# Moving two Strassen products of the last Q unit between the attention tiles of a fused transformer block

## The chip, the cores and the metric

The kernel runs on one core of one Trainium2 chip. The metric is the device time of one execution in microseconds (us). Most executions agree within 0.3%. "Granted clock" below is the mean clock that the throttle gave TensorE in one execution, as a share of full speed. With one core there is no second die to compare with, so a run counts as fast unless it is over 1.5% above the fastest of its kernel; all runs here were fast, apart from one single run whose state is unknown and that is used only for its trace.

## The reference, cut to what matters

```python
def _A_ref(x, wqkv, wo):                 # linear attention, S = 2048, D = 1024, 32 heads
    q, k, v = split(x @ wqkv)
    phi = lambda t: where(t > 0, t + 1, exp(t)) + 1e-6
    pq, pk = phi(q), phi(k)
    kv = einsum("bhsd,bhse->bhde", pk, v)
    z = einsum("bhsd->bhd", pk)
    o = einsum("bhqd,bhde->bhqe", pq, kv) / (einsum("bhqd,bhd->bhq", pq, z)[..., None] + 1e-6)
    return merge_heads(o) @ wo
# _B_ref: (relu(x @ W_gate) * (x @ W_up)) @ W_down, F = 3584
h   = x + _A_ref(layernorm(x), wqkv, wo)
out = h + _B_ref(layernorm(h), W_gate, W_up, W_down)
```

Only the middle of this matters here: Q = layernorm(x) @ wq with phi on it, then for each tile of 128 tokens numerator and denominator ("nd"), the division, the projection with wo, the residual, the second layernorm, and the first products of the FFN.

## The kernel before

All large products are made with seven block products in place of eight (Strassen's scheme in Winograd's form). One *unit* of Q makes two 128-column stripes `v` of the four quadrants. A generator hands out the unit in six pieces, so that the caller can put other work between them. Bank `A` accumulates products 1, 6, 7, 4; bank `E` accumulates 5 and 3. `snap` is a ScalarE copy of a bank as it stands, `fin(i, j, ...)` adds a copy to a bank and starts phi on quadrant (i, j); i = 0 is the first half of the rows. The scheme also needs sums of blocks of its operands, made on VectorE: *left sums* of the tokens and *weight sums* of the weights.

```python
def strassen(pool, work, mm, fin, sbufs=3):
    ...
    yield                                    # products 1, then 2 and 6, came first
    for v in range(2):
        E[v] = pool.tile([P, NW], FP32, tag="E", bufs=2, name="Eq")
        mm(E[v], 5, v, True)
    yield
    for v in range(2):
        mm(A[v], 7, v, False)
        snap(v, "u3")
        fin(1, 1, v, E[v], snaps["u3", v])
    yield
    for v in range(2):
        mm(A[v], 4, v, False)
        fin(1, 0, v, A[v], None)
    yield
    for v in range(2):
        mm(E[v], 3, v, False)
        fin(0, 1, v, E[v], snaps["u2", v])
    yield
```

The second half of the tokens has two Q units, twelve pieces. They are dealt over the eight attention steps 0 to 7. A step runs nd of one tile, the DMA transpose of the quotient of the tile before (`oT`), the projection of the tile two back (`wo_h`), and the DMA transpose and left sums of the tile four back. The first FFN *quad* (`flow`), an early block of the gate and up products by the same scheme, begins in step 8; it reads the sums of tiles 0 to 7. The Q unit that is last feeds tiles 8 to 15: its first-half quadrants tiles 8 to 11, its second-half quadrants tiles 12 to 15.

```python
LAG = (0, 1, 1, 2, 4)                    # nd, oT, x_in, wo_h, hn_T
rest = [p for s in range(1, NS) for c in range(0, KH, 2) for p in [q_unit(s, c)] * 6]
for step in range(QSTEPS):               # QSTEPS = 8
    now = rest[step * len(rest) // QSTEPS:(step + 1) * len(rest) // QSTEPS]
    if step == QSTEPS - 1:
        while now:
            next(now.pop(0))
    attn_step(step)
    ...                                  # early loads of FFN weights
    for p in now:
        next(p)
...
for step in range(QSTEPS, ready):        # steps 8 to 11
    if step == QSTEPS:
        flow.pop(0)()                    # weight sums and first product of FFN quad 0
    attn_step(step)
for n in range(steps):                   # then the rest of flow between the other steps
    attn_step(ready + n)
    ...
```

## Time and profile before

| | before |
|---|---|
| time, median of 3 runs (lowest to highest) | 743.94 us (742.64 to 744.77) |
| span of the profiled execution, granted clock | 740.6 us, 1.0 |
| TensorE (PE) busy | 721.8 us, 97% |
| PE busy of the 127 us from 165 to 292 (attention and early FFN) | 119.98 us |
| start of the first product 5 of FFN quad 0 | 220.34 us |
| start of the later FFN stage (first `accA` product) | 291.11 us |

Read it from the bottom: TensorE does the same matmuls whatever their order, so what can be won is the idle time in the third to last row, 7 us. From 292 us on there is next to none, so the start of `accA` tells nearly the whole of what an edit in this stage does to the end. The lines that carry this are in the prediction.

### The profile page before, as it was taken

To read this page: it belongs to the slowest core of one execution; us is meant where nothing else is said; L and a number is where in the kernel's file an instruction comes from. 1 tells how busy PE (TensorE), PEld (TensorE's weight loads), DVE (VectorE), ACT (ScalarE), POOL (GpSimd) and SP (SyncE) were. 2 spreads that over 40 slices of the span, in tenths; PEclk is the share of its full clock that TensorE was granted. 3 is DMA by queue.
4 is the path that set the end of the run, shared out by engine and by line. 5 is a ranking of instruction groups with operands and counts; after the bars stand their busy time and mean duration, and the time that the engine had idled before them with its cause. 6 is when DMAs were issued, how large, how long until landed. Compare 5 with 4: busy or idle time off the path is not lost.

```text
span 740.6 us, 10570 instructions
## 1 busy us (share of the span) xinstructions
PE 721.8 (97%) x3967; PEld 382.0 (52%) x4020; DVE 563.2 (76%) x991; ACT 322.0 (43%) x580; POOL 5.7 (1%) x44
## 2 busy tenths in 40 slices
PE   7999999999989999999999999999999999999997
PEld 3444555444444444444444444444444458888666
DVE  6997653675887767778778777877787479996797
ACT  4786553778686654444344434443435120000000
POOL 0000000000000000000000000000000000000000
PEclk9999999999999999999999999999999999999999
DMA  9765003079797526164638359475483399988822
GB/s 319 167 140 157 0 1 107 9 155 242 152 223 165 138 73 203 46 181 137 196 127 233 109 181 288 162 221 201 170 271 127 124 396 345 326 286 298 300 79 79
DMA packets 146579, 132.03 MB, mean 178 GB/s; under 512 B 50912, under 2 KB 128096, under 8 KB 146528
## 3 DMA queue, kind: packets, MB, share of 16 engines
q1 hardware_dynamic: 135392, 123.23, 55.3%
q10 hardware_dynamic: 11136, 8.13, 3.4%
q8 instruction: 31, 0.51, 0.3%
q14 instruction: 20, 0.16, 0.1%
HBM read 79.95 MB, written 39.85 MB: 162 GB/s over the span
## 4 chain that ended last, share of the span: by engine, by line
PE 78%; DVE 8%; ACT 7%; DMA 5%; issue 2%; SPq 0%; DVEq 0%; POOL 0%; ACTq 0%
PE accA L785 22%; PE accX L785 8%; PE accY L785 8%; PE accA L1117 8%; PE Aq L298 3%; PE accA L946 3%; PE accX L1117 3%; PE Aq L438 3%; DMA hn<-hn 2%; PE accY L1117 2%; PE attn L541 2%; PE Aq L705 2%; PE Eq L298 2%; PE accY L946 2%; PE accX L946 2%
## 5 line engine op out<-in xcount | busy, mean ns | idle before, releaser
L795 ACT ACTIVATE gu<-gu 128x512 bf16<-128x512 bf16 x72 | 45.4, 631 | 131.5 <-DVE gu L794 131.5
L790 ACT COPY snap<-accA 128x1024 f32<-128x1024 f32 x72 | 72.5, 1008 | 36.3 <-PE accA L785 36.2
L785 PEld LDWEIGHTS <-tg 128*128 128x128 f16 x384 | 37.6, 98 | 45.3
L785 PEld LDWEIGHTS <-tu 128*128 128x128 f16 x384 | 37.6, 98 | 45.3
L541 PE MATMUL attn<-wo_mem,oT 128*128 128x512 bf16 x249 | 57.9, 379 | 1.2 <-DVE o_sb L518 0.4
L794 DVE TENSOR_TENSOR gu<-accY,snap 128x1024 bf16<-128x1024 f32 x36 | 43.9, 1219 | 10.0 <-ACT snap L790 10.0
L785 PE MATMUL accA<-hn,tu 128*128 128x512 f16 (+1 forms) x192 | 49.3, 379 | 0.0
L785 PE MATMUL accA<-hn,tg 128*128 128x512 f16 (+1 forms) x192 | 49.3, 379 | 0.0
L794 DVE TENSOR_TENSOR gu<-accX,snap 128x1024 bf16<-128x1024 f32 x36 | 43.9, 1219 | 6.2 <-PE accX L785 3.7
L154 ACT COPY u<-Aq 128x512 f32<-128x512 f32 x56 | 32.4, 582 | 37.3 <-PE Aq L298 19.3
L1117 PEld LDWEIGHTS <-x 128*128 128x128 f16 (+1 forms) x448 | 43.8, 98 | 5.5
L785 PEld LDWEIGHTS <-wg 128*128 128x128 bf16 x288 | 28.2, 98 | 34.0
L785 PEld LDWEIGHTS <-wu 128*128 128x128 bf16 x288 | 28.2, 98 | 34.0
L541 PEld LDWEIGHTS <-oT 128*128 128x128 bf16 x256 | 24.6, 98 | 30.8 <-issue 2.9
L798 DVE TENSOR_TENSOR hq<-gu 128x512 bf16<-128x512 bf16 x48 | 20.3, 423 | 14.3 <-ACT gu L795 14.2
L298 PEld LDWEIGHTS <-xT 128*128 128x128 bf16 (+1 forms) x192 | 18.6, 98 | 23.7 <-issue 2.3
L1117 PEld LDWEIGHTS <-xs 128*128 128x128 f16 x280 | 27.4, 98 | 3.2
L543 DVE SCALAR_TENSOR_TENSOR x_res<-attn,x_res 128x512 bf16<-128x512 f32 x32 | 21.8, 687 | 7.2 <-PE attn L541 7.1
L946 PEld LDWEIGHTS <-x 128*128 128x128 bf16 (+1 forms) x168 | 16.4, 98 | 19.6
L518 DVE TENSOR_TENSOR o_sb<-nd,rd 128x384 bf16<-128x384 f32 (+1 forms) x48 | 22.8, 507 | 4.5 <-ACT rd L517 4.4
L1123 DVE TENSOR_TENSOR snap<-accA,u 128x1024 f32<-128x1024 f32 x16 | 19.5, 1220 | 8.3 <-PE accA L1117 8.0
L785 PE MATMUL accA<-hn,wu 128*128 128x512 bf16 x96 | 24.6, 379 | 0.0
(232 smaller groups left out, 1400.8 us busy)
## 6 DMA issues: line engine op xcount, KB each, us to landing
x<-x_dram SPq DMA_DIRECT2D x17, 896.0 KB, 8.2
x_dram<-hq SPq DMA_DIRECT2D x28, 512.0 KB, 3.1
wg<-in_B_W_gate_dram SPq DMA_DIRECT2D x14, 512.0 KB, 5.2
wu<-in_B_W_up_dram SPq DMA_DIRECT2D x14, 512.0 KB, 7.3
wraw<-in_B_W_down_dram SPq DMA_DIRECT2D x14, 512.0 KB, 4.8
x_dram<-hq SPq DMA_DIRECT2D x28, 256.0 KB, 2.6
t_dram<-wt SPq DMA_DIRECT2D x28, 256.0 KB, 2.2
xd<-x_dram SPq DMA_DIRECT2D x6, 896.0 KB, 7.1
```

Source lines behind the costliest of these rows:

```text
L154: nc.scalar.copy(out=snaps[nm, v], in_=A[v][:])
L298: nc.tensor.matmul(ps[:], lhsT=left[m - 1][:, kc, r + v * P:r + (v + 1) * P], rhs=right[m - 1][:, kc, :], start=(start and kc == 0), stop= ...
L438: nc.tensor.matmul(ps[:], lhsT=rq[m - 1][:, kc, (c + v) * P:(c + v + 1) * P], rhs=left[m - 1][:, kc, :], start=(start and kc == 0), stop=( ...
L518: nc.vector.tensor_tensor(out=ov[:, c0:c0 + n], in0=ndv[:, :, 0:P].rearrange("p k (h e) -> p k h e", h=HPC), in1=rd[:, 0:n, :].unsqueeze(3 ...
L541: nc.tensor.matmul(ps[:], lhsT=st["oT"][:, c, :], rhs=wo_sb[:, c, j * NW:(j + 1) * NW], start=(c == 0), stop=(c == KC - 1))
L543: nc.vector.scalar_tensor_tensor(out=h_sb[:, j * NW:(j + 1) * NW], in0=ps[:], scalar=1.0, in1=h_sb[:, j * NW:(j + 1) * NW], op0=ALU.mult, ...
L785: nc.tensor.matmul(ps[:, v, :], lhsT=w[v][n - 1][:, kc, :], rhs=left[n - 1][:, kc, :], start=(t is not None and kc == 0), stop=(kc == KH - ...
L790: nc.scalar.copy(out=st[nm][:], in_=halves(st["A"]))
L794: add(out=g[:], in0=halves(st[nm]), in1=st[base][:], op=ALU.add)
L795: nc.scalar.activation(out=g[:, 0, :], in_=g[:, 0, :], func=ACT.Relu)
L946: nc.tensor.matmul(ps[:, t * NW:(t + 1) * NW], lhsT=x_tile(n, s, kh)[:, f, (t0 + t) * P:(t0 + t + 1) * P], rhs=w_tile(n, kh)[:, f, :], sta ...
L1117: nc.tensor.matmul(pv[:, tt, :], lhsT=left(m)[:, f, tt * P:(tt + 1) * P], rhs=right(m)[:, f, :], start=(t is not None and f == 0 and tt % ...
```

## The change

In the last Q unit the first-half quadrants are formed first (products 1, 2, 6, 5, 3), and the two products that only the second-half quadrants need, 7 and 4, are held back to follow attention steps 8 and 9. The intent is to let the tiles of attention start earlier and to give TensorE independent work between them, where it ran dry before. Since product 3 now accumulates onto bank `E` ahead of product 7, product 5 is copied first. The FFN quad begins two steps later.

```diff
-    def strassen(pool, work, mm, fin, sbufs=3):
+    def strassen(pool, work, mm, fin, sbufs=3, late=False):
...
             mm(E[v], 5, v, True)
+            if late:
+                snap(v, "e5", E)
         yield
+        if late:
+            for v in range(2):
+                mm(E[v], 3, v, False)
+                fin(0, 1, v, E[v], snaps["u2", v])
+            yield
+            for v in range(2):
+                mm(A[v], 7, v, False)
+                fin(1, 1, v, A[v], snaps["e5", v])
+            yield
+            for v in range(2):
+                mm(A[v], 4, v, False)
+                fin(1, 0, v, A[v], None)
+            yield
+            return
...
+    last = rest[-2:]
+    del rest[-2:]
     for step in range(QSTEPS):
...
+    for step in range(QSTEPS, QSTEPS + 2):
+        attn_step(step)
+        next(last.pop(0))
...
-    for step in range(QSTEPS, ready):
-        if step == QSTEPS:
+    for step in range(QSTEPS + 2, ready):
+        if step == QSTEPS + 2:
             flow.pop(0)()
```

More of the change, by code (lines that the diff above doesn't have):

```diff
@@ L142, in hold, with snap @@
         nc.gpsimd.tensor_copy(out=dst, in_=src)
-    def strassen(pool, work, mm, fin, sbufs=3):
+    def strassen(pool, work, mm, fin, sbufs=3, late=False):
         A, E, snaps = {}, {}, {}
-        def snap(v, nm):
+        def snap(v, nm, bank=A):
             if v == 0:
@@ L153, in snap @@
             with tc.high_priority():
-                nc.scalar.copy(out=snaps[nm, v], in_=A[v][:])
+                nc.scalar.copy(out=snaps[nm, v], in_=bank[v][:])
         def m2(v):
@@ L447, in fin @@
                 phi_end(pair, e[:])
-        return strassen(pspool, qw[-1], mm, fin)
+        return strassen(pspool, qw[-1], mm, fin, 3, s == NS - 1 and c + 2 == KH)
     with tc.tile_pool(name="qwork0", reuse_waits="tile", bufs=2, side="right") as pool:
```

## The prediction

> **What bounds the kernel now.** I read the page first: TensorE (PE) is busy 97% of the span, and no other engine is near that.
>
> ```profile
> span 740.6 us, 10570 instructions
> PE 721.8 (97%) x3967; PEld 382.0 (52%) x4020; DVE 563.2 (76%) x991; ACT 322.0 (43%) x580; POOL 5.7 (1%) x44
> ```
>
> The reader is to see that all that can be won by moving work, and not removing any, is 740.6 - 721.8 = 18.8 us of idle PE, less than 3%. Next I cut the span by stage (columns: window, its length, busy us and instructions of each engine, clock, DMA share, GB/s).
>
> ```profile
> 120.00:165.00 45.00, 44.76 (x249) 22.00 (x252) 30.45 (x64) 29.95 (x63) 1.05 (x4) 1.00 0.41 106
> 165.00:292.00 127.00, 119.98 (x607) 56.47 (x618) 95.02 (x241) 87.64 (x218) 0.84 (x4) 1.00 0.72 171
> 292.00:580.00 288.00, 286.74 (x1312) 130.61 (x1335) 220.90 (x406) 123.80 (x165) 0.00 (x0) 1.00 0.55 175
> ```
>
> The second row is the attention stage with the second half's Q products and the first early FFN quads: 7.0 us idle. The FFN stage after it has only 1.3 us idle, so whatever reaches it earlier carries through. In ten-microsecond windows the hole is at 210 to 220, where PE is busy 7.28. The timeline of PE there (start, length, line, what; in brackets the idle time before and what ended it; L541 output projection, L511 numerator and denominator "nd", L705 early FFN quad):
>
> ```profile
> 211.75 0.52 PE L511 MATMUL nd<-kvz,pq_mem 128*128 128x132 bf16 x6
> 212.11 0.38 PE L705 MATMUL Dq<-hn,wg 128*128 128x512 bf16 x1
> 212.74 0.28 PE L511 MATMUL nd<-kvz,pq_mem 128*128 128x132 bf16 x2 [0.25 <-DVE o_sb L518]
> ...
> 213.34 3.61 PE L541 MATMUL attn<-wo_mem,oT 128*128 128x512 bf16 x15
> 216.79 0.51 PE L511 MATMUL nd<-kvz,pq_mem 128*128 128x132 bf16 x6
> 218.06 0.28 PE L511 MATMUL nd<-kvz,pq_mem 128*128 128x132 bf16 x2 [0.76 <-DVE o_sb L518]
> 220.34 0.59 PE L705 MATMUL Eq<-hs,tg 128*128 128x512 f16 x2 [2.00 <-DVE hs L117]
> ```
>
> PE has run out of work and waits 0.25, 0.76 and 2.00 us. The last wait is for the sums of token tile 7, the last of the eight that the first FFN quad needs. The chain of waits says where those came from:
>
> ```profile
> 210.50 1.24 ACT hn L553 x2
> 211.84 0.14 ACT sm L554
> 212.01 0.21 ACT sm L555
> 212.24 0.30 ACT sm L556
> 212.57 1.24 ACT hn L557
> 213.81 0.32 ACT den L515 x2
> ...
> 215.62 4.21 DMA hn<-hn
> 219.85 0.44 DVE hs L117
> ```
>
> Normalise (ACT), queue, transpose by DMA, sum (DVE): from the end of tile 7's projection, 207.6 by the PE timeline, to 220.34 it is 12.8 us. PE cannot shorten this chain; it can only start it earlier or have work beside it.
>
> A balance I use below: from the first Q matmul (122.2) to 220.34 are 98.1 us. In them PE does 224 Q matmuls, 160 of projection and 12 of the early quad, 396 x 0.216 us (eight take 1.73 us in the chain) = 85.5 us, and 13 tiles x 8 nd matmuls x 0.059 us (eight take 0.47 us) = 6.1 us. So 91.6 us of work and **6.5 us of idle**: 3.0 in the three waits above, 1.1 where PE waits for an ACT copy at 186.3, 0.3 for a transpose at 203.8, the rest in crumbs.
>
> **What the Trainium skill says.** (1) "TensorE: Matmul & The Clock Gate", in "Wait — 56ns, not 53.3ns?", has warm 512-column matmuls at 215.7 ns start to start; this trace agrees: 1.73 us for eight. (2) "PSUM — Partial Sum Buffer", in "Engine vs sequencer instructions": the queues of ScalarE and VectorE are strict FIFO and matmuls start in program order. So the order of the program decides who waits behind whom; I see nothing in the trace against it. (3) The same page, "PSUM bank collisions raise a hardware error", wants accesses of two engines to one bank guarded by semaphores, ACT reads against PE writes too. Before, product 4 continues on the bank that ACT must first copy; the trace shows that wait, 1.10 us on PE at 186.28 released by the copy. (4) "Perfetto Trace Analysis", in "Per-instruction lifecycle: what the profiler-reported window actually captures": on DMAs the data movement lies outside the slice. Agreed here: the transposes of hn show 1.23 us in the SP queue but 3.2 to 5.1 us to landing, median 3.9 in this stretch. I use the landing.
>
> **The change, part by part.** Nothing is added or removed on PE: its order lists 8042 rows in both kernels.
> - In the last Q unit the order of products becomes 1, 2, 6, 5, 3, 7, 4. ACT copies product 5 (two copies of 0.58 us) instead of the sum before product 7 (two of 0.58): net zero. The exponentials, clamps and adds stay the same in number.
> - Moved: products 7 and 4, 16 matmuls x 0.216 = **3.45 us of PE**, from before attention step 7 to after steps 8 and 9. They feed only tiles 12 to 15, whose nd comes later, so the data allows it.
> - The first early quad begins two steps later (its first product, 8 matmuls, 1.73 us).
>
> I compared the built PE orders. Up to the end of tile 7's projection PE has 82.4 us of work before and 79.0 after: product 4 and the first FFN product (together 3.45) are now behind it. Up to the first product-5 matmul of the quad, where the 2.00 us wait was, both have the same 91.6 us. So after the change PE holds 91.6 - 79.0 = 12.6 us of work beside the tile-7 chain, where before it held 91.6 - 82.4 = 9.2 beside a chain of 12.8.
>
> How long is the chain in its new place? ACT's new order puts two things into it: Square of tile 7 stands behind the two ACT reads of product 4 (done about 2.4 us after the projection ends, where the square could have started at some 1.6), and two FFN copies and one exponential (2 x 0.58 + 1.14 = 2.3 us) come inside. My estimate, from the projection's end: square until 3.6, copies 4.7, exponential and small steps 7.0, normalise 8.2, queue 9.0, landing (3.9) 12.9, sum 0.44: 13.3 us. Minus 12.6 leaves a wait of 0.7 us where 3.0 was: **2.3 us gained**.
>
> Other terms: the 1.1 us copy wait loses its reason in this unit (product 4 now follows long after), but product 3 must now wait for ACT's copy of product 5, and the second of those copies stands behind a square of tile 4: I put +0.3 to +0.5 on it. Tile 8's nd now follows product 3 by 4.1 us of PE work instead of 7.8, while its chain (two DVE adds 1.4, exponential 1.1, clamp 0.4, maximum 0.7, plus hand-overs) is about as long: up to 0.5 us lost. Together +0.2 us gain. Sum: 2.5 us, 743.9 - 2.5 = **741.4 us**.
>
> **Rivals.** (a) *The wait only moves.* Steps 8 to 11 are spaced 4 to 5 us in the trace; with two hn buffers, each square waits for the transpose of two tiles earlier ((3.3 ACT + 1.5 queue + 4 DMA)/2 = 4.4 us). If that ring, and not PE, sets the pace, the filler fits beside it but the tiles come no sooner, and the wait in front of product 5 stays near 2 us: 743.3. For it: DMA share is 1.0 at 160 to 180 and again at 200 to 220. Against it: tile 7 starts 3.45 us of PE work earlier, and tiles 4 to 6 are spaced 4 to 7 us there. (b) *ACT becomes the bound.* It is busy 8.2 to 8.8 of 10 us at 160 to 190, and PE gives up 3.45 us of cover in just those steps, though ACT also gives up some 3.7 us (two exponentials, two reads). If PE then waits for ACT all through steps 3 to 7, the gain halves: 742.7. (c) *It all comes off.* The copy wait goes and the chain is fully covered: 4 us, 739.9. (d) *A slip later.* The early quads after 220 have their own 3.0 us of idle (70.9 us from 220.34 to the first accA matmul, 67.9 of work); the reshuffled order could add one. That would make it 744 to 745.
>
> **Range and chances.** Between (c) and (a) lies 739.7 to 743.7, which I take as the range: low end everything won, high end nearly nothing. Faster by 2% would be 729, more than 14 us gained of 18.8 idle: about nil. Slower by 2% needs 15 us of new waits: nil. So faster 0.01, same 0.98, slower 0.01.
>
> **What would show it right or wrong.** Right: in the changed profile the wait before the first Eq matmul of the early quad is under 1 us, that matmul starts near 217.8 instead of 220.3, PE busy at 210 to 220 rises from 7.3 to above 9, and the start of the first accA product moves from 291.3 to about 288.8. Rival (a) shows as 1.5 us or more in front of that matmul, released by DVE sums that waited for hn; (b) as new PE waits on ACT copies or on nd's inputs between 160 and 200; (d) as more than 3.5 us of idle between that matmul and accA. The prediction is wrong if the gain is there at 220 but not at the end, or if tile 8's nd waits over 1 us.

## More of the kernel before

One more pair of lines from before's timeline of TensorE (start, length, engine, line, what, count) is needed later. They are the projections of tiles 3 and 4; a count of 15 is 16 with one record missing.

```profile
175.27 3.62 PE L541 MATMUL attn<-wo_mem,oT 128*128 128x512 bf16 x15
...
187.57 3.62 PE L541 MATMUL attn<-wo_mem,oT 128*128 128x512 bf16 x16
```

They start 12.3 us apart. Between them PE does most of products 6 and 4, half of 2 and the whole of 5 and 7 of the last Q unit.

## The result, and the profile after

| | before | after |
|---|---|---|
| median (lowest to highest), 4 runs each | 743.38 (742.64 to 744.77) | 740.18 (739.59 to 740.64) |
| ratio of fast runs, 95% interval | 1 | 0.9954 [0.9936, 0.9972] |
| span of the profiled execution | 740.6 | 738.4 |

A ratio is the mean time of one kernel's fast runs over that of the other's of the same rounds, so it is not quite the ratio of the medians. The change gains 0.5%, which is "same" at 2% but clear of zero. Results are correct.

The head of the page after the change:

```profile
span 738.4 us, 10554 instructions
...
PE 722.7 (98%) x3967; PEld 382.2 (52%) x4020; DVE 562.9 (76%) x991; ACT 323.0 (44%) x580; POOL 5.6 (1%) x44
```

TensorE's work is the same; the span is 2.2 us shorter. By stage (window, its length, busy us and instructions of PE, PEld, DVE, ACT, POOL, granted clock, DMA share, GB/s):

```profile
165.00:292.00 127.00, 122.33 (x618) 57.58 (x629) 96.17 (x243) 89.72 (x220) 1.11 (x4) 1.00 0.72 171
210.00:220.00 10.00, 7.69 (x46) 3.70 (x45) 10.00 (x31) 9.16 (x29) 0.00 (x0) 1.00 0.75 133
```

The first row has 2.35 us more PE work in the same window than before. The second shows something that was not forecast: PE is no fuller than before (7.69, from 7.28), and VectorE (DVE), which was busy 7.81 of these 10 us, is now busy for all 10. The timeline of PE after the change says what PE did there (L454 Q products, L527 nd, L557 projection, L726 early FFN quad, L806 the later FFN stage; `x_res` is the residual add, `o_sb` the quotient of a tile, `hs` a left sum):

```profile
156.34 3.61 PE L557 MATMUL attn<-wo_mem,oT 128*128 128x512 bf16 x15 [0.53 <-DVE o_sb L534]
...
170.55 1.89 PE L557 MATMUL attn<-wo_mem,oT 128*128 128x512 bf16 x8 [0.20 <-DVE o_sb L534]
...
176.99 3.62 PE L557 MATMUL attn<-wo_mem,oT 128*128 128x512 bf16 x15
...
182.16 3.61 PE L557 MATMUL attn<-wo_mem,oT 128*128 128x512 bf16 x16
...
202.94 1.89 PE L454 MATMUL Aq<-xT,tq 128*128 128x512 bf16 x8
...
212.09 0.59 PE L557 MATMUL attn<-wo_mem,oT 128*128 128x512 bf16 x2 [1.54 <-DVE x_res L559]
213.16 0.34 PE L527 MATMUL nd<-kvz,pq_mem 128*128 128x132 bf16 x3 [0.48 <-DVE o_sb L534]
...
218.51 0.59 PE L726 MATMUL Eq<-hs,tg 128*128 128x512 f16 x2 [0.30 <-DVE hs L117]
...
288.87 1.03 PE L806 MATMUL accA<-hn,wg 128*128 128x512 bf16 x4
```

Five things are to be seen. Two small waits for VectorE, 0.53 and 0.20 us, are new early in the stage. Tile 4's projection (182.16) now follows tile 3's by 5.2 us in place of 12.3. The last product of the Q unit (202.94) stands between the projections. The wait of 2.00 us before the first `Eq` product has shrunk to 0.30, and that product starts 1.8 us earlier. But two new waits, 1.54 and 0.48 us, stand a little ahead of it, and both are for VectorE. From the `Eq` product on, the start of `accA` has moved from 291.11 to 288.87, and from there to the end both kernels take 449.5 us: what was won stayed won.

The chain of waits of the changed kernel, followed through this place, names VectorE for most of it (start, length, engine, what, line):

```profile
200.41 4.08 DMA hn<-hn
...
204.51 0.43 DVE hs L117
...
206.34 0.61 DVE x_res L559 x2
...
208.07 0.34 DVE tg L635
...
210.42 0.34 DVE tu L641
...
212.64 0.48 DVE o_sb L534
...
215.56 1.35 DVE o_sb L534 x3
216.90 1.22 DVE x_res L559 x4
218.12 0.35 DVE hs L117
```

A transpose of `hn` lands at 204.49; from there to 218.5 the chain is VectorE's own queue, except for two microseconds of PE at 213.2 to 215.2. In the middle are eight weight sums (`tg`, `tu`, 208.07 to 210.76) that the FFN quad asks for when it begins. Before the change they ran between 194 and 200, and the chain there names them only just ahead of a quotient whose transpose PE awaited for 0.29 us. Now they stand just ahead of the residual adds that free the banks for PE's next projections. PE's two waits of together 2.0 us, which the prediction did not have, stand here; whether the weight sums are behind them is tried in the third question.

The balance, by the waits that the two timelines list from the first Q matmul of the second half (122.07 us before, 121.88 after) to the first `Eq` product: before 3.01 us (0.25, 0.76, 2.00), 1.10 for a ScalarE copy and 0.29 for a transpose, together 4.40; after 0.30, 1.54 and 0.48, and the early 0.53 and 0.20, together 3.05. That is 1.35 us less waiting, in a stretch that became 1.63 us shorter (98.26 to 96.63); the rest is in gaps too small to be listed. From `Eq` to `accA` another 0.42 us went (70.78 to 70.36), where the waits listed fell from 1.69 to 1.30. Together the stage took 2.05 us less, 169.04 us before and 166.99 after.

### The profile page after: what moved, and what is told of

It is laid out like the page before. It is cut to its first block, busy times and chain, and to the rows that moved or that the text cites. A ratio compares the mean times of both kernels' runs of the same rounds, so it can differ in the third digit from the quotient of the medians.

```text
span 738.4 us, 10554 instructions
## 1 busy us (share of the span) xinstructions
PE 722.7 (98%) x3967; PEld 382.2 (52%) x4020; DVE 562.9 (76%) x991; ACT 323.0 (44%) x580; POOL 5.6 (1%) x44
## 4 chain that ended last, share of the span: by engine, by line
PE 79%; DVE 10%; ACT 5%; DMA 4%; issue 2%; SPq 0%; DVEq 0%; POOL 0%; ACTq 0%
PE accA L806 22%; PE accY L806 8%; PE accX L806 8%; PE accA L1138 8%; PE attn L557 4%; PE Aq L314 3%; PE accA L967 3%; PE accX L1138 3%; PE Aq L454 3%; PE accY L1138 2%; PE Eq L314 2%; PE accY L967 2%; PE accX L967 2%; ACT hn L569 2%; DMA hn<-hn 1%
## 5 line engine op out<-in xcount | busy, mean ns | idle before, releaser
L557 PE MATMUL attn<-wo_mem,oT 128*128 128x512 bf16 x247 | 58.1, 379 | 3.3 <-DVE x_res L559 1.5
L806 PEld LDWEIGHTS <-tu 128*128 128x128 f16 x384 | 37.6, 98 | 45.3
L806 PEld LDWEIGHTS <-tg 128*128 128x128 f16 x384 | 37.6, 98 | 45.3
L806 PE MATMUL accA<-hn,tu 128*128 128x512 f16 (+1 forms) x192 | 49.3, 379 | 0.0
L806 PE MATMUL accA<-hn,tg 128*128 128x512 f16 (+1 forms) x192 | 49.3, 379 | 0.0
L806 PEld LDWEIGHTS <-wg 128*128 128x128 bf16 x288 | 28.2, 98 | 34.0
L806 PEld LDWEIGHTS <-wu 128*128 128x128 bf16 x288 | 28.2, 98 | 34.0
L557 PEld LDWEIGHTS <-oT 128*128 128x128 bf16 x256 | 24.7, 98 | 33.2 <-issue 5.0
L806 PE MATMUL accA<-hs,tg 128*128 128x512 f16 x96 | 24.6, 379 | 0.0
```

What stands on the lines that cost most here:

```text
L557: nc.tensor.matmul(ps[:], lhsT=st["oT"][:, c, :], rhs=wo_sb[:, c, j * NW:(j + 1) * NW], start=(c == 0), stop=(c == KC - 1))
L806: nc.tensor.matmul(ps[:, v, :], lhsT=w[v][n - 1][:, kc, :], rhs=left[n - 1][:, kc, :], start=(t is not None and kc == 0), stop=(kc == KH - ...
```

## The experiments

Twelve kernels ran. All gave correct results. Times are medians with the lowest and highest run and their number; ratios are against the kernel before, run in the same rounds (744.30, 744.37 and 744.27 us there, 11 runs each).

### First question: which part of the change pays?

The theory of the prediction was *cover*: what counts is how much PE work lies beside the chain of tile 7. Its rival was that the tiles' own pace decides. Four runs take the change apart.

**The change again**, for a level on the same chip.

> The changed kernel unaltered, as the yardstick beside the three variants on the same chip. Theory (cover: what matters is how much TensorE work lies between the end of tile 7's output projection and the first FFN matmul that needs its sums, 12.6 us here against 9.2 before): about 3 us faster than the kernel before, ratio near 0.996, with a wait of 1.5 us on a DVE x_res eviction near 212 us again. Rival (the gain is scatter of runs): ratio within 0.999 to 1.001.

Measured: 740.22 us (739.55 to 741.62, 6 runs), ratio 0.9949 [0.9934, 0.9965]. The gain repeats.

**The new order of products alone.** The two late pieces stay where they were dealt, and the FFN quad begins in step 8.

```diff
-    last = rest[-2:]
-    del rest[-2:]
...
-    for step in range(QSTEPS, QSTEPS + 2):
-        attn_step(step)
-        next(last.pop(0))
...
-    for step in range(QSTEPS + 2, ready):
-        if step == QSTEPS + 2:
+    for step in range(QSTEPS, ready):
+        if step == QSTEPS:
```

> Only the new order of products 1 2 6 5 3 7 4 in the last Q unit; all six pieces stay before attention step 7 and the first FFN quad begins at step 8, as before. By the built order 10.9 us of TensorE work lie beside the tile-7 chain of about 13 us. Cover theory: a wait near 2 us remains in front of the first matmul that needs the sums; the 1.1 us wait on the ACT copy is gone; 1 to 2 us faster than before, ratio 0.9975 to 0.9985. Rival A (the copy wait is the whole gain): as fast as the changed kernel, ratio 0.996. Rival B (only the late placement counts): ratio 1.000.

Measured: 745.87 us (744.97 to 746.37, 6), ratio 1.0019 [1.0003, 1.0034]: alone the new order loses. Its PE timeline shows the price that the prediction had put on it, the wait of product 3 for the copy of product 5 (0.78 us), and late transposes and quotients:

```profile
184.68 1.89 PE L454 MATMUL Eq<-xS,wq_sb 128*128 128x512 f16 x8 [0.78 <-ACT e L154]
...
218.15 3.63 PE L557 MATMUL attn<-wo_mem,oT 128*128 128x512 bf16 x15 [1.79 <-DMA oT<-o_sb]
224.61 3.39 PE L557 MATMUL attn<-wo_mem,oT 128*128 128x512 bf16 x8 [2.27 <-DVE o_sb L534]
```

**The later start of the FFN quad alone**, in the kernel before.

```diff
-        if step == QSTEPS:
+        if step == QSTEPS + 2:
             flow.pop(0)()
```

> Only the other half: the first FFN quad begins at step 10, not 8; the Q products stay in the old order and place. By the built order 13.9 us of TensorE work lie beside the chain. Cover theory: the wait in front of the first matmul that needs the sums is under 1 us although no Q product moved, and the kernel is 2 to 3 us faster than before, ratio 0.996 to 0.9975. Rival B (moved Q products are what fills the hole): nothing filled, ratio 1.000 or slower.

Measured: 743.66 us (743.36 to 746.09, 6), ratio 0.9997 [0.9981, 1.0013]. This is the run that overturns the theory of cover. The first `Eq` product has 13.9 us of PE work beside the chain of tile 7, more than in the change, and indeed PE does not wait there. But it waits elsewhere instead, and nothing is gained. Two of the waits in its PE timeline:

```profile
205.31 0.39 PE L541 MATMUL attn<-wo_mem,oT 128*128 128x512 bf16 x1 [1.05 <-DMA oT<-o_sb]
...
222.06 3.61 PE L541 MATMUL attn<-wo_mem,oT 128*128 128x512 bf16 x16 [1.61 <-DVE o_sb L518]
```

(This profile is of the slowest of the kernel's six executions, at clock 0.998.) PE work behind a wait is no help if other tiles of attention, and not the FFN quad, are what PE runs out of.

**Half of the move**: only product 4 is late (after step 8), and the quad begins in step 9.

```diff
-    last = rest[-2:]
-    del rest[-2:]
+    last = rest[-1:]
+    del rest[-1:]
...
-    for step in range(QSTEPS, QSTEPS + 2):
+    for step in range(QSTEPS, QSTEPS + 1):
...
-    for step in range(QSTEPS + 2, ready):
-        if step == QSTEPS + 2:
+    for step in range(QSTEPS + 1, ready):
+        if step == QSTEPS + 1:
```

> Half the dose: new order, but only product 4 is moved behind step 8, and the quad begins at step 9. By the built order the work beside the chain is 9.2 us, as in the kernel before, because the scheduler put both pieces ahead of tile 7's projection. Cover theory: a wait of 2 to 3 us stays there, and at most the copy wait of 1.1 us is gained, ratio 0.9985 to 1.000. Rival C (gain goes with the amount of work moved late): half the gain of the changed kernel, ratio 0.998.

Measured: 745.73 us (743.96 to 747.35, 6), ratio 1.0019 [1.0001, 1.0036]. Half of the move gains nothing at all. That is odd for any theory in which each product moved brings its 1.73 us. It is not against cover, which expected a wait of 2 to 3 us before the first `Eq` product here: the trace has 1.99, and one of 2.25 us for a transpose at 194.28. Its PE timeline, projections of tiles 3 and 4:

```profile
175.65 3.61 PE L557 MATMUL attn<-wo_mem,oT 128*128 128x512 bf16 x16
...
187.08 3.61 PE L557 MATMUL attn<-wo_mem,oT 128*128 128x512 bf16 x15
```

They are still 11.4 us apart. The likely reason is in the code that deals the pieces: `rest` has 12, 11 or 10 pieces for eight steps, so the steps get 1,2,1,2,1,2,1,2 of them before, 1,1,2,1,1,2,1,2 in this run, and 1,1,1,2,1,1,1,2 after the change. Taking two pieces off the end re-deals *all* the steps, and only with ten does step 5, which stands between the projections of tiles 3 and 4, get one piece instead of two.

### Second question: is it idle PE time that is filled?

Useless matmuls (the projection weights with themselves, result unused) show how much idle time a place has: what they cost less than their own 3.45 us was idle before. In the same job the kernel before was profiled again.

> The kernel before, unaltered, for a second profile: the first was of its fastest execution. Expected: about 744 us, and between the first Q product of the attention stage and the first accA product 9.5 to 11 us of TensorE idle (9.6 in the first profile), with the same three waits: on the ACT copy, and 2 to 4 us in front of the first FFN matmul that needs tile 7.

Measured: 746.44 us, one run, state unknown, granted clock 0.995. The same waits are there, but the last of them, expected at 2 to 4 us, is 1.28 us. The run is used for its trace further down.

**16 useless matmuls in the kernel before**, eight each after steps 8 and 9.

```diff
+    def dummy_mm(n=8):
+        d = pspool.tile([P, NW], FP32, tag="D", bufs=1, name="dummy")
+        for k in range(n):
+            nc.tensor.matmul(d[:], lhsT=wo_sb[:, k % KC, 0:P], rhs=wo_sb[:, k % KC, 0:NW],
+                             start=(k == 0), stop=(k == n - 1))
...
         attn_step(step)
+        if step < QSTEPS + 2:
+            dummy_mm()
```

> The kernel before plus 16 useless matmuls (3.45 us of TensorE at 0.216 each), eight after attention step 8 and eight after step 9, where the changed kernel puts products 7 and 4; their result is not read. Theory 2 (the stretch from tile 7 to the first FFN quad is paced by each tile's own chain of eviction and DMA transposes, so only TensorE work that waits for none of it fits in, and it fits in for nothing): 0 to 1.2 us slower than before, ratio 1.000 to 1.0016. Rival (TensorE is the pace there, and the gain comes from somewhere else): 3.45 us slower, ratio 1.0046.

Measured: 745.76 us (744.86 to 746.06, 6), ratio 1.0018 [1.0002, 1.0033]. 3.45 us of work cost 1.4 us by the medians, so about 2 us of it were hidden. Among the executions of this job with a clock of 0.999 or more the medians are 742.91 (six) and 745.50 us (four): there it cost 2.6 us and only 0.9 were hidden. So there is idle time to fill in that place, but how much this run does not settle; the built order changed too (26 more PE instructions of the trace lie behind the first `accA` product).

**The same in the kernel with the late start of the quad.**

> The late-begin variant plus the same 16 useless matmuls: the shape of the changed kernel around steps 8 and 9, but with work that was not taken from anywhere. Theory 2: the waits on transposes that the late-begin variant showed (2 us in front of projections of tiles 5 to 9) are filled, so nearly no time is added to its 743.7: ratio to before 0.9995 to 1.0015. Rival: 3.45 us added, ratio 1.0043.

Measured: 747.77 us (745.99 to 748.47, 6), ratio 1.0046 [1.003, 1.0062], so 3.4 us above the kernel before and 4.1 above the late start alone (of another job). The expectation that this work would be largely free was missed. It says something useful: this kernel has the late quad *and* as much independent PE work between the tiles as the change has, and none of that work was hidden. Without its 3.45 us this kernel would stand at 744.3, not at 740.2. Work between the tiles is not enough; what is left, by elimination, is that it was taken away from in front of them, and with it the order and dealing of the rest.

**16 useless matmuls in the changed kernel**, after steps 10 and 11.

```diff
+        if step < QSTEPS + 4:
+            dummy_mm()
```

> The changed kernel plus 16 useless matmuls after steps 10 and 11. Its trace shows 2.3 us of waits left there (1.5 on an x_res eviction, 0.5 on o_sb, 0.3 on the sums). Theory 2: the hole has been used up for the most part, so 1.5 to 3.5 us are added to the changed kernel's 740.2: ratio to before 0.997 to 0.9995. Rival D (there is still room of 3 us or more): unchanged, ratio 0.995.

Measured: 745.68 us (745.03 to 747.73, 6), ratio 1.0026 [1.0008, 1.0043], 5.5 us above the changed kernel by the medians, which is 2 us more than the work itself. No idle time shows there that could hide anything; where the extra 2 us come from was not looked into.

### What separates the kernels that gain

With these runs a milestone can be compared over the kernels of the first two questions: when VectorE starts the second residual add of a tile, which follows its projection, counted from the first Q matmul of the second half in the same trace.

| profile | tile 4 | tile 5 | tile 6 | tile 7 | sums of tile 7 | median |
|---|---|---|---|---|---|---|
| before | 69.2 | 78.4 | 81.4 | 86.4 | 97.8 | 744.3 |
| order alone | 68.9 | 81.1 | 82.3 | 89.1 | 102.5 | 745.9 |
| quad late alone | 68.9 | 77.6 | 80.5 | 85.3 | 98.5 | 743.7 |
| half of the move | 68.8 | 78.5 | 81.9 | 91.4 | 101.2 | 745.7 |
| quad late + useless work | 68.7 | 77.2 | 80.2 | 86.0 | 100.4 | 747.8 |
| the change | 64.1 | 72.2 | 76.0 | 84.4 | 96.2 | 740.2 |

Only where both products have left the front do tiles 4 to 6 come earlier, and then by 5 to 6 us. That is the theory that replaces cover: the re-dealt pieces bring tiles 4, 5 and 6 forward, and the two products kept back fill PE while tiles 6 to 8 go through their chains. It fits every row. But it was argued from the traces and not tried by itself: a kernel that deals the pieces anew and keeps both products early was not run. Nor are early tiles enough: the kernel with useless work in the change and those of the third question, which all have both products late, start tile 4 at 64.1 to 64.8 and tile 6 at 76.0 to 76.9, and three of these five (pool opened first, gate sums early, sums on GpSimd) have no gain left in the median. What is also to be read from the table: of the 5.4 us that tile 6 has in hand, tile 7 keeps 2.0 and its sums 1.6. Product 7, which still stands ahead of tile 7's projection (8 matmuls from 197.29), takes part of the rest; more is lost on VectorE, in the chain shown above, where the second add of tile 7 starts at 206.26, 3.2 us after the projection has ended at 203.1.

### Third question: can VectorE's queue be relieved?

**Weight sums behind the step's own work.** The quad begins after step 10's attention work and not ahead of it.

```diff
     for step in range(QSTEPS + 2, ready):
+        attn_step(step)
         if step == QSTEPS + 2:
             flow.pop(0)()
-        attn_step(step)
```

> The changed kernel with the first FFN quad begun just after attention step 10 instead of just before it. On VectorE five of the eight weight sums (0.335 us each) now stand behind the x_res eviction of tile 8 on which TensorE waited 1.5 us; all eight still stand ahead of the sums of tile 7. Theory 3 (VectorE as a whole is the new bound there, it is busy 10.0 of the 10 us from 210 to 220): the wait on x_res falls below 0.5 us, but as much comes back in front of the first matmul that needs tile 7; ratio to before 0.9945 to 0.9965, as the changed kernel (0.9951). Rival (only the position of the sums counts): 1 to 1.5 us faster than the changed kernel, 0.993 to 0.9938.

Measured: 740.13 us (739.56 to 740.80, 5), ratio 0.9946 [0.9933, 0.996], against 0.9949 [0.9934, 0.9965] for the change: no difference can be told. The profile is the best of all: the wait of 1.54 us for the residual add is gone, PE is busy 9.15 of the 10 us from 210 to 220, and the first `Eq` product starts 0.9 us earlier:

```profile
211.27 1.07 PE L527 MATMUL nd<-kvz,pq_mem 128*128 128x132 bf16 x8 [0.30 <-DVE o_sb L534]
...
217.62 0.59 PE L726 MATMUL Eq<-hs,tg 128*128 128x512 f16 x2 [0.41 <-DVE hs L117]
```

So with five of the eight weight sums moved behind that add its wait is gone from the trace: that wait came of VectorE's queue. The stage is about 1 us shorter (166.05 us against 166.99 and 167.87 in the two profiles of the change), but that microsecond is not shown to be the weight sums': tile 7's second add, ahead of all of them, already starts 1.0 us earlier than in the change (83.4 us after the first Q matmul, by the measure of the table, in place of 84.4), behind a transpose that lands 0.9 us earlier. In the median of whole executions nothing shows.

**Memory of the weight sums opened ahead of the second half's buffers**, so that it lies in space that is free sooner, and, in a second kernel, also the gate sums of quad 0 made in step 5 in a small pool of their own.

```diff
-    new_hn(1)
     tpool = mctx.enter_context(tc.tile_pool(name="tpool", reuse_waits="tile", bufs=2))
+    new_hn(1)
```

> The changed kernel with the pool of the weight sums opened ahead of the new hn tiles, so at other addresses. On VectorE the eight weight sums then stand between the first and the second x_res eviction of tile 8. Theory 3: nothing gained, ratio 0.9945 to 0.9965. Position rival: TensorE's wait moves to the second projection half, 0 to 1 us gained.

Measured: 743.85 us (742.47 to 745.32, 6), ratio 0.9996 [0.9981, 1.0011].

```diff
+        if step == 5:
+            steps, ops = weight_sums(early[0][0], 0, "tg", t0pool)
+            for f in steps:
+                f()
+            sums0.append(ops())
```

> As the run with the pool opened first, but four of the eight weight sums of the first quad (those of the gate weights) are made at attention step 5, in a tile of their own, where VectorE is busy only 6.4 of 10 us. Theory 3: 4 x 0.335 = 1.34 us leave the stretch in which VectorE is the bound, so 0.8 to 1.4 us faster than the changed kernel, ratio to before 0.9930 to 0.9940. Rival (the transposes set the pace and VectorE only seems full): no faster than the changed kernel, 0.995.

Measured: 744.06 us (741.29 to 745.74, 6), ratio 1.0 [0.9979, 1.002]. Both were expected to be no slower than the change, and both gave back some 3.6 to 3.9 us. The traces show that opening the pool earlier made the remaining sums *later* (they start at 214.6 and 213.6 us, in place of 208.0), and both have a wait of 1.5 us on a ScalarE copy at 268 and 266 us, which is 0.29 us in the second profile of the change (the run with the quad late alone has one of 1.6 us there too). The stage is 1.2 to 1.4 us longer in their profiles than in the first of the changed kernel, less than the loss. The rest goes with the clock, which the last question is about: at clock 1.0 the first of these kernels took 742.47 us (one run) and the second 741.29 and 741.81, against a median of 740.12 for the change, and the others, at lower clocks, took more. In the profile of the first the stage begins 2.6 us late after a drop of the clock between 10 and 20 us; with its 1.4 us that is the whole of its longer span (742.5 against 738.4). Why these kernels have the lower clock more often is left open.

**Weight sums of quads 0 and 1 on GpSimd**, which is idle.

```diff
-        tt = nc.vector.tensor_tensor
+        tt = (eng or nc.vector).tensor_tensor
...
-            st["q"] = early_quad(0, f, run_sums(early[f // GP], f % GP))
+            st["q"] = early_quad(0, f, run_sums(early[f // GP], f % GP, nc.gpsimd if f < 2 else None))
```

> The changed kernel with the weight sums of the first two quads on GpSimd, which is idle: sixteen instructions leave VectorE, eight of them ahead of tile 7's sums. Theory 3 alone would say 2 us faster than the changed kernel, 0.9925. The SBUF page of the Trainium skill says that VectorE and GpSimd share a port pair that is locked for a whole instruction: if that bites, VectorE instructions of two SBUF inputs get longer (left sums from 0.42 us to over 1 us) and the gain is lost: 0.995 or slower.

Measured: 747.78 us (746.83 to 748.79, 5), ratio 1.005 [1.0035, 1.0064]. The timeline of this kernel, VectorE and GpSimd (POOL) side by side:

```profile
206.99 1.34 POOL L640 TENSOR_TENSOR tg<-wg 128x512 f16<-128x512 bf16 x1
...
207.37 1.25 DVE L119 TENSOR_TENSOR hn<-hn,hn 128x512 f16<-128x512 bf16 x1
...
208.54 1.37 DVE L120 TENSOR_TENSOR hs<-hn,hs 128x512 f16<-128x512 bf16 x1
...
217.03 1.01 PE L557 MATMUL attn<-wo_mem,oT 128*128 128x512 bf16 x2 [5.91 <-DVE x_res L559]
```

A left sum on VectorE (L119, L120) takes 0.42 us in the changed kernel and 1.25 to 1.37 us here. The Trainium skill, "SBUF — State Buffer", section "Who interferes with whom", says that VectorE instructions with two SBUF inputs contend with GpSimd instructions that read SBUF, by way of a port pair that they share. This run agrees: VectorE is not relieved but slowed threefold, and PE waits 5.91 us for it.

### A term that no timeline of the first pair had: the clock

The first profiled execution of the kernel before (742.45 us) was the fastest of its job and had a granted clock of 1.0. Most of its executions do not. The second profile of it shows what happens (window, length, busy PE, PEld, DVE, ACT, POOL, granted clock, DMA share, GB/s):

```profile
221.00:223.00 2.00, 0.32 (x3) 0.20 (x3) 2.00 (x9) 1.97 (x7) 0.00 (x0) 0.86 0.73 152
223.00:225.00 2.00, 2.00 (x5) 0.67 (x5) 2.00 (x7) 1.77 (x6) 0.00 (x0) 0.50 0.72 145
225.00:227.00 2.00, 2.00 (x9) 0.82 (x8) 1.56 (x4) 1.22 (x4) 0.00 (x0) 0.78 1.43 274
```

In the same hole in front of the first `Eq` product, the clock falls to half just as PE gets its work, and stays down for some three microseconds: 5 matmuls in 2 us, where the next window at full clock (227 to 229) has 11. The same drop shows in the order-alone run (0.57 at 224 to 226), in half of the move (0.72 at 195 to 200), in the second profile of the change (0.81 at 215 to 220) and behind the long wait of the GpSimd run (0.50 at 215 to 220). Three of the fourteen profiles (this one, the quad late alone and the pool opened first) also have a drop in the prologue, to 0.83 between 10 and 20 us, long before the part that the edits touch. In them the first Q matmul of the second half starts at 124.3 to 124.5 us, in all others at 121.9 to 122.4. In this second profile of the kernel before, 2.5 of the 4.1 us by which its span is longer than the first lie ahead of that matmul, and 1.6 in the stage behind it: the larger part of that loss is not the hole's.

Over the three jobs of experiments: of 33 executions of the kernel before, 24 have a granted clock of 0.998 or less, with a median of 744.56 us, and nine have 1.0, with a median of 742.82. Of the ten executions of the change listed in this document, seven have 1.0 (median 740.12) and one is below 0.999. So among runs at full clock the change gains 742.82 - 740.12 = 2.7 us, and the rest of what the medians show, 4.1 us, comes with executions of the kernel before that had a lower clock and took 1.7 us more. That a fuller hole trips the clock less often is a reading of these counts and not shown; how many of the 24 drops lay in the hole and how many in the prologue only their traces could tell, and there is one, which has both.

## Why the prediction was right

The time was forecast at 741.4 us (739.7 to 743.7) and came to 740.18; "same" at 2% was right. The hole of 7 us, the place of it and that moving work could win 2 to 3 us of it were right. How they were won was right only in part, and that the sum came so close is luck in part. By its own steps:

- *Wait before the first Eq product under 1 us, product near 217.8 us.* Right and nearly right: 0.30 us, 218.51 us.
- *accA from 291.3 to about 288.8 us.* Right, with a start misread by 0.2: from 291.11 to 288.87 us. (The first Q matmul, put at 122.2, starts at 122.07.)
- *The copy wait goes.* Right: 1.10 us gone. *Product 3 waits for the copy of product 5, +0.3 to +0.5.* Not in the change, where no such wait is listed; 0.78 us of it where the order alone was changed.
- *Rival (a), the wait only moves.* Partly: 2.0 of the 3.0 us moved, to VectorE's residual add and quotient and not to the ring of `hn` buffers that this rival had named.
- *Tile 8's nd loses up to 0.5 us.* No such wait is in the trace; two that no term had are, 0.53 and 0.20 us for quotients at 156.34 and 170.55. Nor did rivals (b) and (d) show: no new ScalarE wait, and `Eq` to `accA` takes 70.4 us, not more than the 70.8 before.
- *12.6 us of work beside a chain of 13.3: 0.7 us of wait for 3.0.* The term that was mis-sized. The chain of tile 7 took 15.4 us, from the end of its projection (203.1) to the end of its last-needed sum (218.46). The square was to end 3.6 us after the projection and ended after 5.5, because tile 7's second residual add stood in VectorE's queue behind a sum of an earlier tile that waited 1.89 us for its transpose. Normalise was to end after 8.2 us and ended after 9.4, and from there to the sum it was 6.0 us in place of 5.1: the transpose took 4.7 us (212.89 to 217.60) and not 3.9, and the sum then stood 0.4 us in VectorE's queue. In the same stretch PE waited 1.54 and 0.48 us for VectorE before it could do the work that was to lie beside the chain. I had counted ScalarE's queue instruction by instruction and taken VectorE's as free.
- *PE busy above 9 in 210 to 220.* Wrong for that reason, 7.69. With the weight sums behind the step it is 9.15.
- So the waits at the end of the stage gave 0.7 us and not 2.3 (3.01 to 2.32). The other listed waits up to `Eq` gave another 0.7 and not 0.2 (1.10 and 0.29 gone, 0.53 and 0.20 new), and 0.4 us came behind `Eq`, where none was forecast. With the small gaps that makes the 2.05 us of the stage and 2.2 of the span: close to 2.5 from terms that were off in opposite ways.
- *The argument of cover itself* did not hold as put: the late start of the quad alone had 13.9 us of cover and gained nothing. The other half of the same sentence, that PE can start the chain earlier, is the half that agrees with the table of milestones, though no run tried it alone. I had seen 3.45 us less work ahead of tile 7 and missed that the dealing of the pieces brings tiles 4 to 6 five to six microseconds forward.
- *The clock* was no term at all: the forecast took 2.5 us from a median that holds runs at a lower clock. At full clock the gain is 2.7 us, very near; the medians show 3.2 and 4.1.

## What to carry to other kernels

When independent work is moved between the stages of a pipeline, list the queue of every engine on the chain in its new place, not only that of the busiest: here VectorE, which was 78% busy beside the old hole, was the one that set the new wait. Where pieces of work are dealt over steps by a division, removing one at the end shifts all of them; compare when each tile reaches a fixed milestone before and after. And before a gain of half a per cent is explained, divide the runs by their granted clock.

## What the Trainium skill lacked or had wrong

- "TensorE: Matmul & The Clock Gate", "Why this matters for your kernels", asks for no idle gaps over about 3 us between bursts of matmuls. Here no single wait was longer than 1.28 us in the hole of the second profile of before (0.32, 1.00 and 1.28 us between 219.7 and 222.95, with short matmuls among them), and the granted clock still fell to 0.50. That is nearer to what the page's section "A second HAM failure mode: psum-queue depth-cycling" tells of micro-idling; the row of advice by itself would not have warned of this gap. In the first profile a wait of 2.00 us in the same hole left the clock at 1.00. The page tells of variation from run to run for the warm-up at a kernel's start; that the same program falls in the middle of one run and not of another, and what it costs, it does not tell. Here 24 of 33 executions had a clock of 0.998 or less, and the medians of the two sorts lie 1.7 us apart (the drops in the prologue among them).
- "SBUF — State Buffer", "Who interferes with whom", has the contention but no length for this pair of operations. Here both engines, given 128x512 sums at the same time, started one about every 1.3 us, where VectorE alone starts one every 0.34 us.
